# Attention V mixed with the mixing matrix stationary and gathered through DRAM, six exponent buffers, second mean on VectorE

## The chip, the cores and the metric

The kernel runs on one core of a Trainium2 chip. The metric is the device time of one execution in microseconds (us). Most executions of one kernel agree within a few tenths of a per cent; one of the first three of the kernel before took 669 us, is far outside, and is not used. Where kernels are compared, the runs were made in turns on the same chip and only runs of the fast state count.

## The reference, cut to what matters

Four batches of attention with eight heads, 768 tokens and 64 columns. The tokens fall into 8 blocks of 96, and a Sinkhorn-normalised 8 x 8 matrix P for each batch and head mixes the blocks of K and V before block-local attention. The result goes through a Fourier mix, a layer norm and a feed-forward network (512 to 2048 to 512).

```python
for _ in range(5):
    P = P - np.max(P, axis=-1, keepdims=True); P = np.exp(P)
    P = P / (np.sum(P, axis=-1, keepdims=True) + 1e-09)
    P = P / (np.sum(P, axis=-2, keepdims=True) + 1e-09)
k_sorted = np.einsum('bhij,bhjcd->bhicd', P, k_b)
v_sorted = np.einsum('bhij,bhjcd->bhicd', P, v_b)      # the change is about this line
attn = softmax(scale * q_b @ k_sorted.T)               # in blocks of 96
out = attn @ v_sorted                                  # then Fourier mix, layer norm, FFN
```

## The kernel before

A list scheduler in Python orders all operations ahead of time from estimated costs; every engine then works through its own list in order. V comes in two halves: batches 0 and 1, then 2 and 3. V arrives with (batch, head, block) on the 128 partitions. The products need the 96 tokens of a block on partitions. The kernel before gets there on TensorE: V is copied so that 96 tokens of one column d lie side by side, that piece is the stationary operand, and the mixing matrix `bd` streams past it.

```python
# V's path, t = 0 or 1 for the half
for hf in range(2):                       # mean over tokens, on TensorE
    for n in range(6):
        nc.tensor.matmul(psm.ap, idh, nat[t][:, 3072*hf + 512*n : ... + 512], ...)
V.tensor_reduce(vb[:, 0, :], psm.ap.rearrange("p (c d) -> p d c", d=D), ...)
# ... 8 pieces: t=0 a copy, t=1 minus the mean, both to "p (d r c)"
V.tensor_tensor(dst, src, vbn[...].broadcast_to([128, 16, 6, 8]), op=ALU.subtract)
# mixing: 64 stationary operands, 128 columns stream past each
nc.tensor.matmul(o, vcx[:, 96*d : 96*d + m], bd, ...)
copy(e, vsb[0:96, :, 4*n : 4*n + 4], ps.ap[0:96].rearrange("p (d g) -> p g d", d=4))
# ...
# exponent buffers, zeroed once by GpSimd
for n in range(4):
    nc.gpsimd.memset(eb4[0:96, n, :], 0.0)
# layer norm's small steps on GpSimd, between the loads that GpSimd issues
G.tensor_scalar(mv.ap[:, :, 1], mv.ap[:, :, 1], 1e-6, None, op0=ALU.add)
# results of the second token group go out by GpSimd's row scatter
nc.gpsimd.indirect_dma_start(out..., bass.IndirectOffsetOnAxis(ap=rows[:, i:i+1], axis=0), u.ap, None)
```

Loads with a cast from float32 to float16 are issued by GpSimd. So GpSimd's one list holds loads, buffer fills, layer-norm steps and row scatters.

The softmax here doesn't subtract the row's maximum and nothing guards it: scores larger than these inputs give would overflow.

## Time and profile before

| | before |
|---|---|
| time, two runs | 290.75 and 292.56 us |
| first feed-forward product (ff1) starts | 70.25 us |
| last product's result added | 281.57 us |
| TensorE / VectorE / ScalarE / GpSimd busy | 260.9 / 171.9 / 157.9 / 66.3 us |

Busy time by engine, and two of the 40 slices that the prediction does not show, from the page of the kernel before (7.25 us a slice, busy share in tenths):

```profile
PE 260.9 (90%) x2284; PEld 155.2 (54%) x2284; DVE 171.9 (59%) x405; ACT 157.9 (54%) x323; POOL 66.3 (23%) x104
...
POOL 8973300015900640011220002032000212200021
PEclk9997999998899999999999999999999999999997
```

GpSimd (POOL) is empty in the sixth to eighth slice and nearly so in the ninth, up to 65 us, just before the layer norm of batch 0 falls due at 64 us, and TensorE's granted clock (PEclk) is under 8 tenths in one slice only, the fourth. When that layer norm falls due, GpSimd is waiting for its statistics, not they for it (start, us, instruction, idle before it and what ended it):

```profile
64.33 0.26 POOL L1193 TENSOR_SCALAR mv<-mv 128x3 f32<-128x3 f32 x1 [25.71 <-DVE mv L1188]
```

I use one more quantity, TensorE's **lag**: the time at some point minus the work that TensorE has done up to it. The work is each matmul in its list times the steady spacing of its shape, 0.162 us for 384 columns and so on, as the prediction derives them. Counted row by row by one rule for all kernels, it is 236.9 us before. The lag is 34.3 us when ff1 starts and 44.6 at the end. It grows where TensorE waits or runs at half clock.

### The profile page before, as it was taken

To read this page: it belongs to the slowest core of one execution; us is meant where nothing else is said; L and a number is where in the kernel's file an instruction comes from. 1 tells how busy PE (TensorE), PEld (TensorE's weight loads), DVE (VectorE), ACT (ScalarE), POOL (GpSimd) and SP (SyncE) were. 2 spreads that over 40 slices of the span, in tenths; PEclk is the share of its full clock that TensorE was granted. 3 is DMA by queue.
4 is the path that set the end of the run, shared out by engine and by line. 5 is a ranking of instruction groups with operands and counts; after the bars stand their busy time and mean duration, and the time that the engine had idled before them with its cause. 6 is when DMAs were issued, how large, how long until landed. Compare 5 with 4: busy or idle time off the path is not lost.

```text
span 290.0 us, 5807 instructions
## 1 busy us (share of the span) xinstructions
PE 260.9 (90%) x2284; PEld 155.2 (54%) x2284; DVE 171.9 (59%) x405; ACT 157.9 (54%) x323; POOL 66.3 (23%) x104
## 2 busy tenths in 40 slices
PE   0389988897999999999999999999999999999980
PEld 0258866554565656554566456455555546545530
DVE  4697999999999999831579643145034226210020
ACT  2677979785778945970477037137415505425300
POOL 8973300015900640011220002032000212200021
PEclk9997999998899999999999999999999999999997
DMA  7999999910990897211113010311311111221001
GB/s 114 211 260 245 215 208 211 219 37 5 157 146 10 95 165 133 66 37 20 77 47 57 36 52 22 58 72 50 57 72 37 38 54 72 38 90 36 2 36 72
DMA packets 42529, 26.33 MB, mean 91 GB/s; under 512 B 30106, under 2 KB 38824, under 8 KB 42500
## 3 DMA queue, kind: packets, MB, share of 16 engines
q0 software_dynamic: 23536, 18.31, 37.4%
q1 hardware_dynamic: 18966, 7.64, 11.6%
q8 instruction: 18, 0.29, 0.4%
q14 instruction: 9, 0.07, 0.1%
HBM read 28.96 MB, written 6.29 MB: 122 GB/s over the span
## 4 chain that ended last, share of the span: by engine, by line
PE 62%; DVE 22%; DMA 8%; issue 3%; POOL 2%; ACT 1%; POOLq 0%; DVEq 0%
PE bank L1253 26%; PE bank L1274 25%; DMA hr<-in_v_dram 4%; DVE vsf L660 3%; DVE vcx L708 3%; DVE rt L1006 3%; DMA out_dram<-u,rows 2%; POOL kq L472 2%; DMA kq<-in_q_dram 2%; PE bank L1149 2%; PE bank L991 2%; DVE st L1186 1%; PE bank L952 1%; PE bank L897 1%; DVE ks L660 1%
## 5 line engine op out<-in xcount | busy, mean ns | idle before, releaser
L1265 ACT ACTIVATE hr<-bank 128x384 f16<-128x384 f32 x115 | 56.3, 491 | 75.2 <-PE bank L1253 74.4
L1253 PE MATMUL bank<-ut,w1sb 128*128 128x384 f16 x512 | 92.8, 329 | 0.7 <-ACT ut L660 0.7
L1274 PE MATMUL bank<-w2sb,hr 128*128 128x512 f16 x384 | 87.9, 379 | 0.0
L1253 PEld LDWEIGHTS <-w1sb 128*128 128x128 f16 x512 | 49.0, 99 | 34.8 <-issue 1.8
L1274 PEld LDWEIGHTS <-hr 128*128 128x128 f16 x384 | 36.7, 98 | 41.8 <-issue 0.2
L1282 DVE TENSOR_TENSOR u<-bank,u 128x512 f32<-128x512 f32 x24 | 16.5, 689 | 60.2 <-PE bank L1274 59.8
L961 ACT ACTIVATE ex<-bank 96x384 f32<-96x384 f32 x64 | 27.9, 485 | 6.3 <-PE bank L952 6.0
L1295 POOL DMA_INDIRECT out_dram<-u,rows x12 | 12.2, 1013 | 77.0 <-DVE u L1282 56.7
L1193 POOL TENSOR_SCALAR mv<-mv 128x3 f32<-128x3 f32 x8 | 1.9, 240 | 109.8 <-DVE mv L1188 109.8
L976 ACT ACTIVATE eb<-ex,negone 96x384 f16<-96x384 f32 x35 | 20.8, 615 | 0.2
L1213 ACT ACTIVATE un<-u,nm,ny 128x512 f16<-128x512 f32 x15 | 12.2, 810 | 11.8 <-DMA ut<-un 8.5
L1172 DVE SCALAR_TENSOR_TENSOR u<-rt,bank 128x510 f32<-128x510 f16 x12 | 8.1, 678 | 16.3 <-PE bank L1138 8.9
L991 PE MATMUL bank<-vsf,eb 97*128 97x65 f16 x416 | 16.5, 193 | 1.3 <-DVE rr L836 0.5
L1006 DVE TENSOR_TENSOR rt<-bank,rz 128x384 f16<-128x384 f32 x32 | 17.2, 549 | 0.3
L991 PEld LDWEIGHTS <-eb 97*128 97x128 f16 x416 | 15.4, 98 | 3.6 <-issue 1.3
L472 POOL DMA_DIRECT2D kq<-in_q_dram x20 | 16.4, 850 | 1.7 <-DMA kq<-in_q_dram 1.2
L1186 DVE BATCH_NORM_STATS2 st<-u 128x6 f32<-128x512 f32 x24 | 16.1, 686 | 0.3
L1160 DVE SCALAR_TENSOR_TENSOR u<-rt,bank 128x512 f32<-128x512 f16 x12 | 8.0, 684 | 13.9 <-PE bank L1153 13.5
L927 PE MATMUL bank<-pack,qr 128*128 128x128 f16 x48 | 4.8, 246 | 12.3 <-ACT qr L660 11.7
L724 PE MATMUL bank<-bdv,vcx 128*128 128x128 f16 (+1 forms) x128 | 12.6, 225 | 0.0
L952 PE MATMUL bank<-qt,ks 64*128 64x96 f16 x256 | 11.3, 207 | 1.3 <-DVE rt L1006 0.4
L897 PE MATMUL bank<-bdk,kq 128*64 128x128 f16 x192 | 10.7, 228 | 1.6 <-DVE bdk L636 0.8
(130 smaller groups left out, 338.2 us busy)
## 6 DMA issues: line engine op xcount, KB each, us to landing
kq<-in_k_dram POOLq DMA_DIRECT2D x8, 384.0 KB, 6.6
w1sb<-in_moe_w_ch_dram POOLq DMA_DIRECT2D x4, 512.0 KB, 16.0
w2sb<-in_moe_w_ch_dram POOLq DMA_DIRECT2D x4, 512.0 KB, 19.0
out_dram<-u SPq DMA_DIRECT2D x8, 256.0 KB, 2.0
kq<-in_q_dram POOLq DMA_DIRECT2D x4, 384.0 KB, 11.6
hr<-in_v_dram POOLq DMA_DIRECT2D x2, 768.0 KB, 11.2
kq<-in_v_dram POOLq DMA_DIRECT2D x2, 768.0 KB, 21.5
kq<-in_q_dram POOLq DMA_DIRECT2D x16, 96.0 KB, 5.5
```

The source lines that it names most:

```text
L472: o = P.add({eng: c}, lambda _: e.dma_start(dst, src), r=r, w=w, prio=prio, nbytes=nbytes, tag="load", after=after)
L897: nc.tensor.matmul(ps.ap[64 * h2:64 * h2 + 64, 128 * r3:128 * r3 + 128], k16[:, 2 * hl + h2, 3 * half + r3, :], bdk[:, 2 * hp + h2].rearra ...
L952: nc.tensor.matmul(pss[h2].ap[:, BLK * j:BLK * j + BLK], ks.ap[rows, 4 * g + j, :], qt.ap[rows, c0:c0 + BLK])
L961: nc.scalar.activation(ex.ap, pss[h2].ap[0:96, 0:384], AF.Exp, scale=SCALE),
L976: nc.scalar.activation(ed, src, AF.Identity, bias=negone[0:96])
L991: nc.tensor.matmul(po.ap[:, 65 * T:65 * T + 65], eb.ap[:, e0:e0 + 128], vsf[:, vi:vi + 65], start=(n == 0), stop=(n == len(WIN[T]) - 1), s ...
L1006: P.add({"DVE": (0.45, 0.56)}, lambda _: V.tensor_tensor(rt.ap[:, :, D * h:D * h + D], po3()[:, :, 0:D], rz.ap[:, :, None].broadcast_to([1 ...
L1186: P.add({"DVE": (0.6, 0.69)}, lambda _, u=u, st=st: V.bn_stats(st.ap, u.ap), r=[u], w=[st], tag="bn")
L1253: nc.tensor.matmul(ps.ap[:, 0:GT], w1sb[:, c, 128 * fc:128 * fc + 128], ut.ap[:, c, :], start=(c == 0), stop=(c == 3))
L1265: nc.scalar.activation(hr[g][:, fc, :], ps.ap[:, 0:GT], AF.Relu)
L1274: nc.tensor.matmul(ps.ap, hr[g][:, fc, 128 * tt:128 * tt + 128], w2sb[:, fc, :], start=(fc == 0), stop=(fc == 15))
L1282: V.tensor_tensor(u.ap, ps.ap, u.ap, op=ALU.add),
```

## The change

Its intent: no copies of V, fewer and larger products, contiguous evictions. The mixing matrix becomes stationary and V streams past it, 512 columns at a time. The result still has (batch, head, block) on partitions; it is stored to DRAM and gathered back with tokens on partitions. The gathers stand on GpSimd's list, the load queue. Two more exponent buffers are to bridge the trip, and the second half's mean moves to VectorE.

```diff
+VW = 80
+NEB = 6
...
+            for n in range(4):                      # second half's mean
+                P.add({"DVE": (1.65, 1.75)}, lambda _, n=n: V.tensor_reduce(
+                    vb[:, 0, 16 * n:16 * n + 16],
+                    n3.rearrange("p c d -> p d c")[:, 16 * n:16 * n + 16],
+                    axis=AX.X, op=ALU.add), ...)
...
+        for hf in range(2):                         # centring, in place
+                V.tensor_tensor(m, m, vbn[:, None, :].broadcast_to([128, 48, D]), op=ALU.subtract)
...
-                    nc.tensor.matmul(o, vcx[:, 96 * d:96 * d + m], bd, ...)
+                nc.tensor.matmul(o, bd, n4[:, r, 8 * hf:8 * hf + 8], start=True, stop=(t == 1))
...
+                      nc.sync.dma_start(vdr[t][w64, cols], vm[w64, cols]),
...
+                          nc.gpsimd.dma_start(
+                              vsb[32 * k_:32 * k_ + 32, w64, 0:D],
+                              vdr[t][w64, cols].rearrange("g (c d) -> c g d", d=D)),
...
+    gate = gets[0, 0][-1:]                          # tables and weights behind the first gathers
```

Less visible parts: V is loaded first, its second half in six pieces instead of two; the pieces that spread the mixing matrix are split into a high and a low half.

## The prediction

> **What bounds the kernel now.** I read the page's slices first, then the chain that ended last, then busy time by stage, then the groups by shape, then the timelines of VectorE and TensorE. The page's 40 slices (7.25 us each, tenths busy):
> ```profile
> PE   0389988897999999999999999999999999999980
> ...
> DVE  4697999999999999831579643145034226210020
> ACT  2677979785778945970477037137415505425300
> ...
> DMA  7999999910990897211113010311311111221001
> ```
> VectorE (DVE) is full from the fourth slice to the sixteenth, TensorE (PE) from the ninth to the end. The transfers are dense to about 58 us. Busy time by stage (a stretch in us, its length, then PE, PEld, DVE, ACT, POOL busy):
> ```profile
> 27.00:66.00 39.00, 34.18 (x581) 26.64 (x579) 38.39 (x95) 33.78 (x73) 4.86 (x10) 1.00 0.96 176
> 66.00:92.00 26.00, 23.74 (x208) 15.37 (x207) 25.11 (x61) 18.97 (x38) 10.31 (x15) 0.93 0.84 85
> 92.00:115.00 23.00, 22.55 (x305) 13.77 (x302) 22.56 (x49) 16.04 (x35) 8.09 (x10) 1.00 1.03 122
> 115.00:277.00 162.00, 161.89 (x1055) 87.98 (x1050) 65.43 (x148) 73.11 (x152) 18.68 (x33) 1.00 0.19 50
> ```
> From 27 to 66 us VectorE works 38.4 of 39 us: this front is VectorE's. From 115 to 277 us TensorE is busy 161.9 of 162 and VectorE 40%: that part is TensorE's. The chain of work that ended last says the same (start, us, what), with the start of the first feed-forward product, ff1, and the end of the last product:
> ```profile
> 36.43 0.62 DVE rr L836
> 37.32 0.47 DVE rt L1006
> ...
> 70.25 2.14 PE bank L1253 x8
> ...
> 277.24 0.70 DVE u L1282
> ```
> So the end is: TensorE's work, plus the time it has nothing to do, plus 12.8 us of closing (277.2 to 290.0). Busy time overstates its work, as matmuls overlap, so I count work by the steady spacing of blocks in the chain: 24 ff1 matmuls in 3.90 us (0.162 each), 36 ff2 in 7.77 (0.216), 26 attention matmuls in 0.80 (0.031), 16 of V's mixing in about 0.9 (0.056). Multiplied over the instruction order of TensorE this gives 240 us in all, 38.3 before the first ff1 and 56.4 before the first ff2 (which runs at 92.6 us). TensorE is thus without work for 70.25 - 38.3 = 32 us before ff1, 36 us by 92.6, and 277.2 - 240 = 37 us in all. The gain can come from two terms only: the 240, and the 37.
>
> **What the Trainium skill says, and whether the trace agrees.** "VectorE: DVE Perf Modes", The perf-mode tier table: a tensor_tensor on 16-bit SBUF operands reaches 2x, a tensor_reduce[...] 1x. The trace agrees for a dense one (pmt, 768 elements, 545 ns, against 800 ns for one element a cycle at the page's 0.96 GHz) and shows that the strided centring of V does not (768 elements in 1473 ns). "TensorE: Matmul & The Clock Gate", Back-to-back issue gap: N/2.4 + 2.5 ns, so 128 columns 56 ns and 512 columns 216; the blocks above agree with both. "DMA: Bandwidth & Descriptors", Anatomy of one DMA: some 2 us fixed in each transfer, and (Specifications) pieces under 512 B are slow. Here a plain 256 KB store lands in 2.0 us, and q loads of 768 rows of 256 B (96 KB) in 5.5. "SBUF — State Buffer", Terms: VectorE and GpSimd exclude each other on a shared port pair, which could delay the gathers' descriptors; no view of the kernel before shows that.
>
> **The change, part by part.** The groups by shape that it touches (busy us, mean ns):
> ```profile
> L724 PE MATMUL bank<-bdv,vcx 128*128 128x128 f16 x126 | 12.4, 225 | 0.0
> L708 DVE TENSOR_TENSOR vcx<-kq,vbn 128x768 f16<-128x768 f16 x8 | 11.7, 1473 | 0.0
> L660 ACT CAST vsf<-bank 96x512 f16<-96x512 f32 x16 | 11.6, 791 | 0.4 <-PE bank L724 0.3
> L660 DVE CAST vsf<-bank 96x512 f16<-96x512 f32 x16 | 11.4, 774 | 1.2 <-PE bank L727 1.1
> ...
> L727 PE MATMUL bank<-bdv,vbn 128*128 128x128 f16 x63 | 8.3, 231 | 0.0
> ...
> L660 DVE COPY vcx<-hr 128x768 f16<-128x768 f16 x5 | 4.5, 941 | 0.7 <-DMA hr<-in_v_dram 0.7
> L660 ACT COPY vcx<-hr 128x768 f16<-128x768 f16 x3 | 4.5, 1499 | 0.2 <-DMA hr<-in_v_dram 0.2
> ...
> L675 PE MATMUL bank<-kq,pack 128*128 128x512 f16 x12 | 2.9, 380 | 0.0
> ```
> *TensorE.* Out: 128 + 64 mixing matmuls of 128 columns at 0.056 = 10.8 us, the 12 of the second mean at 0.216 = 2.6, eight fp32 ones (about 1.3). In: 36 of 512 columns at 0.216 = 7.8, and 24 small fp16 ones (about 1.2). Net -5.7 us. All of it counts, since TensorE's work adds up to the end: the new order sums to 234.3.
>
> *VectorE.* I take durations from like rows and counts from the two instruction orders. Out: 16 evictions 11.4, centring 11.7, copies 4.1 (0.8 apart), one PSUM mean 0.7, small 1.3: 29. In: 9 evictions of 512 contiguous at about 0.62 = 5.6; two centrings of 3072 at 2x, 3072/1.92 GHz + 0.06 = 1.66 each, 3.3; four reductions of 1536 at 1x, 1.66 each, 6.6; four more exponent shifts and six more ReLUs taken from ScalarE (4.5); two q copies and the split of the mixing matrix in two halves (2.5): 22.5. Net -6.6 us. *ScalarE:* 16 evictions and 3 copies out, 15 evictions at 0.55 in, 10 pieces handed to VectorE: about -14 us.
>
> *Before the first normalised tile.* VectorE's order up to it (66.2 us in the kernel before) loses 5 copies (4.1), 10 evictions against 5 (3.7), 4 head norms and a matrix copy of the next batch (3.7), gains about 2.7: 8.8 us less. Also, one Sinkhorn exponential waited 2 us for q's copy on ScalarE; now the five run together, 1.76 us an iteration, so the mixing matrix is ready at about 11.6 instead of 14.3 us.
>
> *The new wait.* V is loaded first. Its halves landed 3.7 us apart (12.7 and 16.4) after k and q; without those (3.7 us together) I expect 9.0 and 12.7. Behind V, q lands at 14.6 and k at 16.4, and TensorE's order has q's transposes and one product of k ahead of the mixing: start 17.4. 12 steps of 0.43 and evictions end near 23. The last store of the first half is out at 23.5 and lands at 27. A gather moves 2048 rows of 128 B; two k loads and eight q loads (6144 rows) took 10.7 us (70.9 to 81.6), less 3.7 for k is 1.14 ns a row, so 2.3 us a gather, plus 2 fixed: last gather at 32 to 34 us. The six exponent buffers let three pairs of heads be ready by then. VectorE's own order ahead of the first head norm, 17.6 us from 17.4, says 35. The kernel before did that norm at 36.3. So the round trip costs about nothing, and from the norm to the first normalised tile VectorE has 22.8 us of work left (30 before). First ff1: 35 + 22.8 + 1 + 4 (66.2 to 70.25 before) = 62.8.
>
> *Sum.* Idle before ff1: 62.8 - 32.6 (work in the new order) = 30.2, so 1.8 less. Idle after it was 5 us; with looser engines I take 3.5. Work -5.7. In all -9 us: 292.6 to 283.5.
>
> **The rivals.** (1) **The round trip becomes the wait.** Stores and gathers meet k, q and the tables in queues that were full to 58 us; if the last gather lands at 38 or 40, ff1 starts at 67 and the gain falls to 5 us or less: 287 to 289. For it: dense transfers, 12,288 tiny rows a half. Against: tables and weights are held behind the first gathers. (2) **Weights arrive late.** They are issued after the gathers, some 10 us later than now (21.5 to 33 us). By bytes I expect w1 by about 54 and w2 by 63 us, in time; if not, ff1 waits: 286 to 290. (3) **GpSimd's in-order queue.** Gathers of the second half stand ahead of the row scatters of batch 0 and between layer-norm steps; a late store would hold those and, through the six u buffers, TensorE: 1 to 4 us at about 100 us. (4) **More gain.** The front was VectorE's from 27 on; if it simply shifts by 8.8 us and the 5 us behind it vanish, 277 to 280.
>
> **Range and chances.** The work term (-5.7) is firm to a microsecond. The start of ff1 is loose by 3 us either way, the stalls behind by 2. Quadratically some 4 us; with rival 3 the upper side is longer: 277 to 290. Faster by over 2% means under 286.7, 3.2 us above the centre: 0.69. Slower by 2% (298) needs a stall that I don't see: 0.05.
>
> **What would show it.** Right: first ff1 near 63 us and first head norm near 35; V's 36 mixing matmuls 0.216 apart; centring near 1.7 us; VectorE near 165 and ScalarE near 144 us busy; no TensorE gap of a microsecond after ff1. Wrong: TensorE's first attention product waiting for a gather with VectorE idle (rival 1), ff1 waiting for a weight transfer (2), a vector step waiting for a scatter (3), or a centring or reduction of V far above 1.7 us.

## The result, and the profile after

The changed kernel took 305.7 us (305.39 to 306.31, four runs) against 291.5 us (290.75 to 292.56, three runs, the one of 669 us left out) of the kernel before in the same rounds. The ratio is 1.0486, 95% interval 1.044 to 1.0532: slower. Ratios here are the mean time of one kernel's fast runs over that of the other's of the same rounds, so not quite the ratio of the medians.

| | before | predicted | after |
|---|---|---|---|
| time, us | 291.5 | 283.5 | 305.7 |
| TensorE's work, us | 236.9 | 5.7 less | 231.8 |
| first head norm, us | 36.3 | 35 | 39.8 |
| first ff1, us | 70.25 | 62.8 | 76.59 |
| lag at first ff1 / at the end, us | 34.3 / 44.6 | | 45.8 / 63.3 |
| VectorE / ScalarE busy, us | 172 / 158 | 165 / 144 | 177 / 146 |

The work fell as predicted, by 5.1 us. The lag rose by 18.7. Page of the changed kernel, busy time and slices of 7.6 us:

```profile
PE 259.8 (86%) x2124; PEld 147.1 (49%) x2124; DVE 176.8 (58%) x405; ACT 145.7 (48%) x307; POOL 87.6 (29%) x122
...
PE   0569786824999999799699999999999999999990
...
DVE  5898999735799999755599914316414315310020
...
POOL 8941953445820006762112000212200212200012
PEclk9979797985799999999799999999999999999996
DMA  7996999999990436999421111131221032131001
```

VectorE was full from 29 to 116 us before; now it has a hole in the ninth to eleventh slice, 61 to 83 us, where TensorE drops to 2 and 4 tenths and its clock to 5 in one slice. GpSimd is busy there, and transfers are dense to 91 us (58 before). What TensorE waited for, from its waits (total us, times, longest):

```profile
PE bank L717 <- DMA hr<-in_v_dram: 9.9, 2, 8.9
PE bank L1304 <- DVE u L1253: 8.4, 1, 8.4
PE bank L664 <- DVE fo L643: 3.0, 1, 3.0
PE bank L1325 <- DVE u L1354: 2.9, 2, 2.6
PE bank L1020 <- ACT ex L1029: 1.9, 2, 1.7
```

The first is V's first load, from the start. The other four are the places to look into. Three readings give a cause each.

**The layer norm.** The 8.4 us are a wait for the first normalised tile. GpSimd's timeline of the changed kernel (start, us, instruction, idle before it):

```profile
67.98 1.14 POOL L486 DMA_DIRECT2D kq<-in_v_dram  x1 [1.57 <-DMA w2sb<-in_moe_w_ch_dram]
69.20 0.25 POOL L1265 TENSOR_SCALAR mv<-mv 128x3 f32<-128x3 f32 x1
```

The statistics of batch 0's first group were complete near 61.8 us. The layer norm's first step starts at 69.20, right after the last of six loads of V's second half. Those stand ahead of it in GpSimd's list, and they wait for earlier weight loads: five of the six are issued about 0.5 us after one of these lands (54.6 and 55.1, 57.1 and 57.6, 62.0 and 62.6, 64.7 and 65.3, 67.4 and 68.0 us). Afterwards TensorE runs at half clock. Busy time by stage (length, then TensorE, weight loads, VectorE, ScalarE, GpSimd, then the granted clock, transfer share and GB/s):

```profile
60.00:70.00 10.00, 2.31 (x54) 1.87 (x53) 3.62 (x9) 2.81 (x7) 5.29 (x6) 0.82 1.23 209
70.00:80.00 10.00, 7.52 (x79) 5.44 (x80) 7.04 (x22) 4.87 (x8) 6.26 (x12) 0.50 2.33 162
```

**The start.** The Sinkhorn iterations ended at 11.5 us, as predicted. The next instruction on VectorE spreads the matrix with a copy, and takes 5.80 us. From the two engines' timelines:

```profile
11.55 5.80 DVE L643 COPY fo<-rv 32x1024 f16<-32x1024 f16 x1
...
9.49 7.32 POOL L560 MEMSET eb<- 96x1672 f16 x5
```

Beside it GpSimd fills the exponent buffers, now six of them.

**The second half.** Groups by shape of the changed kernel (busy us, mean ns):

```profile
L706 DVE TENSOR_REDUCE vb<-kq 128x16 f32<-128x1536 f16 x4 | 11.0, 2780 | 0.0
L742 DVE TENSOR_TENSOR kq<-kq,vbn 128x3072 f16<-128x3072 f16 x2 | 3.5, 1759 | 0.0
```

Centring is what the prediction said (1.76 against 1.66 us); a reduction takes 2.78 us instead of 1.66. And from the chain that ended last, a row scatter of batch 0:

```profile
138.52 7.42 DMA out_dram<-u,rows
```

It took 7.42 us to land; the median of all is 2.8. VectorE waits for it because it frees a buffer, and TensorE waits for VectorE at 148 us.

### The profile page after: what moved, and what is told of

The parts are those of the page before. It is cut to its first block, busy times and chain, and to the rows that moved or that the text cites. A ratio compares the mean times of both kernels' runs of the same rounds, so it can differ in the third digit from the quotient of the medians.

```text
span 303.3 us, 5530 instructions
## 1 busy us (share of the span) xinstructions
PE 259.8 (86%) x2124; PEld 147.1 (49%) x2124; DVE 176.8 (58%) x405; ACT 145.7 (48%) x307; POOL 87.6 (29%) x122
## 4 chain that ended last, share of the span: by engine, by line
PE 47%; DMA 4%; DVE 1%; issue 1%; POOLq 0%; DVEq 0%
PE bank L1325 21%; PE bank L1346 20%; DMA out_dram<-u,rows 4%; PE bank L1220 1%; PE bank L1132 1%; PE bank L1059 1%; PE bank L1020 1%; PE bank L1224 1%; DVE u L1354 0%; POOLq L1465 0%; PE bank L965 0%; PE bank L1208 0%; PE bank L1137 0%; DVE u L1244 0%; PE bank L1142 0%
## 5 line engine op out<-in xcount | busy, mean ns | idle before, releaser
L1325 PE MATMUL bank<-ut,w1sb 128*128 128x384 f16 x512 | 94.5, 331 | 3.1 <-DVE u L1354 2.9
L1337 ACT ACTIVATE hr<-bank 128x384 f16<-128x384 f32 x109 | 53.3, 490 | 73.1 <-PE bank L1325 72.4
L1367 POOL DMA_INDIRECT out_dram<-u,rows x12 | 12.1, 1007 | 72.7 <-DVE u L1354 57.2
L787 POOL DMA_DIRECT2D vsf<-vdr x12 | 13.0, 1088 | 43.0 <-DMA vdr<-kq 31.1
L1044 ACT ACTIVATE eb<-ex,negone 96x384 f16<-96x384 f32 x31 | 18.5, 614 | 0.3
L1059 PE MATMUL bank<-vsf,eb 97*128 97x65 f16 x416 | 17.2, 198 | 1.4 <-DVE rt L1075 0.5
L1020 PE MATMUL bank<-qt,ks 64*128 64x96 f16 x256 | 12.4, 211 | 2.6 <-ACT ex L1029 1.9
L693 ACT CAST ks<-bank 128x384 f16<-128x384 f32 x18 | 8.1, 482 | 11.6 <-PE bank L965 11.0
```

Source lines behind the costliest of these rows:

```text
L787: nc.gpsimd.dma_start(vsb[32 * k_:32 * k_ + 32, w64, 0:D], vdr[t][w64, cols].rearrange("g (c d) -> c g d", d=D)),
L1020: nc.tensor.matmul(pss[h2].ap[:, BLK * j:BLK * j + BLK], ks.ap[rows, 4 * g + j, :], qt.ap[rows, c0:c0 + BLK])
L1044: nc.scalar.activation(ed, src, AF.Identity, bias=negone[0:96])
L1059: nc.tensor.matmul(po.ap[:, 65 * T:65 * T + 65], eb.ap[:, e0:e0 + 128], vsf[:, vi:vi + 65], start=(n == 0), stop=(n == len(WIN[T]) - 1), s ...
L1325: nc.tensor.matmul(ps.ap[:, 0:GT], w1sb[:, c, 128 * fc:128 * fc + 128], ut.ap[:, c, :], start=(c == 0), stop=(c == 3))
L1337: nc.scalar.activation(hr[g][:, fc, :], ps.ap[:, 0:GT], AF.Relu)
```

## The experiments

Four theories: (A) the layer norm is late by GpSimd's in-order list; (B) VectorE's copies and GpSimd's fills shut each other out; (C) the second mean on VectorE is on the path; (D) the second half's trip makes TensorE wait behind 100 us. The standing rival is the prediction's first: the trip as such, and full transfer queues, set the pace whatever is done about the lists. Sixteen kernels ran. Each ratio is to the kernel before, on the same chip in the same rounds.

### The spreading copy as a maximum (e1)

```diff
-        V.tensor_copy(pk..., phl[0]...broadcast)
+        V.tensor_tensor(pk..., phl[0]...broadcast, phl[0]...broadcast, op=ALU.max)
```

> The changed kernel with one instruction replaced: the copy on VectorE that spreads the mixing matrix (5.80 us at 11.55 us, beside GpSimd's fills of the exponent buffers) becomes an elementwise maximum of the matrix with itself, same result, two inputs. Every engine's order stays the same. Theory (the copy and the fills shut each other out): the maximum takes 1.1 to 1.4 us although the fills still run until 16.8, V's mixing starts near 17 instead of 20.6 us, the first head norm comes 3 to 4 us earlier than 39.84. Rival (the copy is slow by its shape, or the partition range is slow): still 5 us or more. The end: if GpSimd's queue holds the first layer norm (69.2 us) whatever VectorE does, the total moves by less than 2 us: 303.5 to 306; if the start is on the path, about 302.

Measured: ratio 1.0469 (1.0422 to 1.0517), first ff1 at 76.22 us. VectorE's timeline of this run:

```profile
11.72 1.21 DVE L643 TENSOR_TENSOR fo<-rv 32x1024 f16<-32x1024 f16 x1
13.35 3.72 DVE L655 COPY rr<-rv 32x1024 f16<-32x1024 f16 x1
```

Same size, same place, same fills beside it: 1.21 us. The next plain copy, which took 0.4 us in the changed kernel after the fills, now starts among them and takes 3.72, to 17.07. So (B) holds: a copy that meets the fills ends with them, whichever copy it is. This agrees with the Trainium skill, "SBUF — State Buffer", Who interferes with whom: a copy in a two-port mode and a GpSimd instruction exclude each other, and an instruction with two SBUF inputs contends only with a GpSimd instruction that reads SBUF; a fill reads nothing. The start gained less than I expected, since the second copy took the place of the first: mixing began at 19.5 us (17 expected, 20.6 without the edit), and the first head norm at 39.1, 0.7 us earlier instead of 3 to 4. The total did not move, as the layer norm stood at 68.8 us still.

### Layer norm ahead of V's loads (e2), and both (e3)

```diff
-        for o in P.schedule():
+        seq = P.schedule()
+        vl = [o for o in seq if o.n in vloads]      # the six loads of V's second half
+        seq = [o for o in seq if o not in vl]
+        at_ = seq.index(lns[0]) + 1                 # behind batch 0's first layer norm
+        seq[at_:at_] = vl
+        for o in seq:
```

No other engine's order changes.

> The changed kernel with the six loads of V's second half moved on GpSimd's queue to just behind the first layer norm of batch 0; every other order the same. Theory (the layer norm stood behind loads that waited for their turn in the transfer queue): the layer norm starts within 0.5 us of its statistics, near 62 instead of 69.2 us; the 8.4 us wait of TensorE for the first transposes falls to 1 to 2 us; TensorE keeps its full clock between 70 and 80 us (0.50 now); first ff1 near 68 instead of 76.6; total 296 to 299. Rival (weights late, or the statistics themselves late): first ff1 moves by under 3 us and the total stays at 303 to 306. Second rival: V then arrives late for its reductions at 90 us, and half of the gain is lost.

Measured: ratio 1.0292 (1.0233 to 1.035), first ff1 at 70.45 instead of 76.59 us. GpSimd's timeline:

```profile
63.14 0.25 POOL L1267 TENSOR_SCALAR mv<-mv 128x3 f32<-128x3 f32 x1 [8.80 <-DVE mv L1262]
...
65.19 6.94 POOL L486 DMA_DIRECT2D kq<-in_v_dram  x6 [0.22 <-issue]
```

Now GpSimd waits for the statistics, not they for it; TensorE's waits for the first tile are 1.4 and 1.1 us. (A) is shown. Its worth is 1.9%, some 5.7 us; I had expected 7 to 10, and a full clock between 70 and 80 us, where it was 0.83.

> Both edits of the two runs before in one kernel. Theory: the gains add, since with the queue freed the start is on the path: first ff1 near 64 to 65 us, total 292 to 295. Rival (round trip of V through memory, or w1, w2 late, as the prediction's first and second rivals): first ff1 no earlier than with the queue edit alone.

Measured: ratio 1.0271 (1.0227 to 1.0314), first ff1 at 68.99. Together they gain little more than the queue edit alone. The expectation of 292 to 295 failed. The lag tells why: 38.2 us at ff1 and about 42 when the products of the third result tile are done (101.6 us; as much before, at 114.9), but 57.2 at the end (44.6 before). By then the front has been made up for; some 15 us are lost behind it.

### The second mean back on TensorE (e4), and alone on the kernel before (b7)

```diff
-            for n in range(4): ... V.tensor_reduce(... 1536 elements ...)
+            for hf in range(2): ... 6 x nc.tensor.matmul(psm.ap, idh, nat[t][... 512]) ...
```

> The changed kernel with one part undone: the second mean of V again as 12 products of 512 columns on TensorE and one reduction, instead of four reductions of 1536 elements on VectorE (11.0 us). Many orders behind 85 us change with it. If the VectorE reductions hold the path (VectorE is full from 90 to 104 us): VectorE 10 us less busy, idle of TensorE behind the first ff1 (12.4 us) down by 4 or more, total 301 to 303 in spite of 2.6 us more of TensorE's work. If they are hidden: 306 to 308, TensorE's added work.

Measured: ratio 1.0563 (1.0511 to 1.0616). The interval overlaps that of the changed kernel, but in the same rounds it took 309.8 us against 306.3 of e1, so nothing was gained. VectorE is 10.5 us less busy, V's second half is mixed by 110 us instead of 116. But TensorE meets a new wait of 3.9 us at 139.9 us. VectorE waited 4.4 us there for the transposes by transfer of batch 1's normalised tiles.

The same part alone, on the kernel before (the reverse edit):

> One part of the change alone, on the kernel before: the second mean as four reductions on VectorE instead of 12 products on TensorE. By the rows seen: 2.6 us of TensorE's work out, 11.0 us of VectorE's in, between 92 and 115 us where VectorE was busy 22.6 of 23 us. If VectorE has slack there that its order can use: 290 to 292. If V's second half, late by some 8 us, holds TensorE: 293 to 298.

Measured: ratio 1.0379 (1.0341 to 1.0417), about 11 us slower, beyond what I expected. The lists shift around it as well: ff1 starts 2 us later already, and the lag grows to 60.5 at the end. So the part is bad where it stands alone, and undoing it in the changed kernel does not give the time back. (C) can't be settled as a number that adds to others.

### No trip in the second half (e5)

The mean on TensorE, centring in place, V itself as the stationary operand at a stride of 128 bytes, evicted straight to tokens on partitions; e3's two edits kept.

```diff
+                        nc.tensor.matmul(ps.ap[0:128, 128 * dd:128 * dd + 128],
+                            kf[:, d:d + 64 * 127 + 1:64], bd, start=True, stop=True)
```

> The queue edit and the maximum instead of the spreading copy, as in the run with both edits, and in the second half of V no round trip: mean on TensorE, centring in place, then V itself as the stationary operand, read with a stride of 128 bytes (nothing copied), evicted straight to keys on partitions, as the kernel before has it. First half as in the changed kernel. Theory (the second round trip makes TensorE wait between 105 and 158 us: in the run with both edits TensorE falls 13 us behind its work there, the kernel before 3 to 4): it now falls behind by 4 to 6 us, no wait of a microsecond behind 100 us, total 292 to 295. Rival (the loss there comes from the finer interleaving of small products, not from the trip): still 10 us or more and 299 to 302. Side question: a strided stationary operand may load slower than the 106 to 117 ns of others; if it is over 200 ns, mixing is bound by it, 64 loads, some 7 us.

Measured: ratio 1.0386 (1.0306 to 1.0467). No gain in the total. Between 103 and 158 us TensorE falls some 10 us behind (by a recount of the lag), against 13.5 in e3 and 4 before; the theory wanted 4 to 6, the rival 10 or more. No wait of 1.4 us is left there, and the clock is full. The strided weight load takes 201 ns, dense ones of 128 columns 96 to 118. So the trip looks like a few microseconds of the loss behind 103 us, not like most of it, and (D) in its first form falls. The run also moves the mean and lengthens the weight loads, so it doesn't price the trip alone; the rival named in its expectation, the finer interleaving of small products, got no run of its own.

### The gathers of the second half left out (e6)

```diff
+        drop = gets[1, 0] + gets[1, 1]
+        seq = [o for o in seq if o not in drop]
```

Its output is wrong, which doesn't matter for the time.

> Wrong on purpose (batches 2 and 3 read the V of batches 0 and 1): the run with both edits, same order on every engine, with only the six gathers of the second half left out. It asks what the second trip's last step costs by itself. Theory: the 2.75 us wait of TensorE at 120 us, the half clock behind it and the slow landings of transposes and row scatters near 135 to 145 us go; TensorE falls behind by about 5 us instead of 13 between 103 and 158; total 292 to 295. Rival (the gathers are hidden; reductions, centring and stores are what costs): total within 2 us of 300.9. Output is wrong.

Measured: ratio 1.0306 (1.0234 to 1.0379), as with them. The gathers are hidden, and my theory was wrong. The run shows the wait more clearly, in three timelines (TensorE, ScalarE, the store queue):

```profile
125.77 0.85 PE L1024 MATMUL bank<-qt,ks 64*128 64x96 f16 x8 [4.52 <-ACT ex L1033]
...
124.53 0.81 ACT L1289 ACTIVATE un<-u,nm,ny 128x512 f16<-128x512 f32 x1 [5.66 <-DMA ut<-un]
...
116.18 10.38 SPq L1300 DMA_TRANSPOSE ut<-un  x3
```

TensorE waits for exponentials. They stand on ScalarE behind a normalisation, which waits for a tile buffer. The buffer is held by a transpose that a transfer does. Before, batch 3's k and q were loaded at 96 to 104 us. Here they run from 114 us, beside these transposes, because V's second half is staged in their slots until its last store.

### Batch 3's loads left out (e10), transposes on TensorE (e8)

> Wrong on purpose (batch 3 reads what lies in its k and q slots): the run with both edits, same order on every engine, with only the ten loads of k and q of batch 3 left out. New theory, after the gathers of the second half turned out to cost nothing: V's second half is staged in the slots that batch 3's k and q need, until its last store, so these loads run at 114 to 131 us instead of 96 to 104, just beside the transposes by transfer of batch 1's normalised tiles; these land late, ScalarE waits 5.7 us for a buffer of such a tile, the exponentials behind it wait, TensorE waits 2.7 to 4.5 us and runs at half clock behind. Theory: transposes land in under 3 us, TensorE's wait at 120 us goes, it falls behind by 5 to 7 us between 103 and 158 instead of 13; total 294 to 297. Rival (the tiles themselves are late, or there are too few buffers whatever the traffic): wait stays over 2 us, total 300 to 302. Output is wrong.

Measured (wrong results): ratio 1.0186 (1.0149 to 1.0224), 0.9% under e3 (on another chip). ScalarE still waits 3.9 us for a transpose, TensorE still 2.8 us at 125 us. The loads have a part in it; the wait does not go with them.

```diff
-            if b > 0:      # transposes by transfer
+            if b > 1:      # batch 1 on TensorE as well
```

> The run with both edits, with the normalised tiles of batch 1 transposed on TensorE as batch 0's are, instead of by transfers on the store queue (24 more products of 0.06 us, some 1.5 us of TensorE's work, six more evictions). Theory (the transfers' landing beside batch 3's loads holds ScalarE): ScalarE's wait for these transfers near 118 to 124 us goes, TensorE's wait for exponentials falls under 1 us, no half clock near 125, total 296 to 299. Rival (the wait only changes its name): 300 to 303.

Measured: ratio 1.0352 (1.032 to 1.0384). This is slower than e3. The rival was right: the wait changes its name. The wait near 123 us is gone, but TensorE waits 3.6 us at 144 us for VectorE, which waited 4.9 us at 141 for a row scatter.

### Six buffers against four (e7)

> The changed kernel with four exponent buffers instead of six. A dose for the theory that VectorE's copies and GpSimd's fills shut each other out: two fills of 1.5 us fewer, so the fills end near 13.9 instead of 16.8 us and the spreading copy that starts at 11.55 ends there too: 2.7 to 3.2 us instead of 5.8. If the copy is slow by itself it stays at 5.8. The total: with four buffers fewer pairs of heads are ready when the gathers land; if six buffers were worth what the prediction says, the first feed-forward product is late by 2 to 4 us although the start is 3 us earlier: 305 to 309; if they are worth nothing, 303 to 306.

Measured: 305.8 to 310.9 us, two of four runs slow, so no ratio. As a dose for (B) it is clean. VectorE's and GpSimd's timelines:

```profile
11.68 2.79 DVE L643 COPY fo<-rv 32x1024 f16<-32x1024 f16 x1
...
9.50 4.43 POOL L560 MEMSET eb<- 96x1672 f16 x3
```

Two fills fewer, and the copy ends at 14.47 instead of 17.35 us, still with the fills. In its profiled run the first attention product waits 4.5 us for a gather, which it did not with six buffers, not even in b3, where mixing started as early (17.2 against 17.6 us): they do bridge the trip. But ff1 came at 72.06 us, 4.5 us earlier than with six buffers, where I had expected it 2 to 4 us later.

### Candidates: both maxima (b3), and the scatter ahead of four loads (b5)

b3 is e8 with the second spreading copy as a maximum and three tile buffers.

> A candidate for a better kernel: as the TensorE-transposes run, with the second spreading copy of the mixing matrix as a maximum too (it took 3.72 us beside the fills) and three buffers of normalised tiles. Expected: mixing of the first half starts another 2 us earlier, first head norm at 36 to 37 us, first feed-forward product at 66 to 67, total 293 to 297. If the landing of stores and gathers in full queues sets the start, the norm stays at 38 to 39 and the total within 1 us of the TensorE-transposes run.

Measured: ratio 1.0227 (1.02 to 1.0253). First head norm at 35.5 us, first ff1 at 66.7: in this run the front is as early as expected, and the total is not. The profiled runs of b4, b5 and b6, with both maxima too, had the norm at 37.5 to 38.6 and ff1 at 67.9 to 69.8, although b5's lists are the same up to there: one profiled run places the front to 2 or 3 us, no better. b5 changes one place in GpSimd's list:

```diff
+        sc = next(o for o in seq if o.tag == "out" and o.eng == "POOL")   # first row scatter
+        # ... the last four q loads of batch 3 go behind it
```

> The candidate with the two maximum instructions, transposes on TensorE and three tile buffers, and one change of GpSimd's order: the first row scatter of batch 0 stands ahead of the last four q loads of batch 3 instead of behind them. In that candidate the tile was ready at 126.1 us, the scatter issued at 128.7 and landed near 136.6 (7.9 us, median 2.7), VectorE waited 6.5 us for its buffer, TensorE 5.2 us and ran at half clock behind. Theory (the prediction's third rival, the in-order queue, and the loads' traffic beside it): scatter issued near 126.4, lands by 130 to 132, TensorE's wait at 132 to 138 us falls to 0 to 2 us, no half clock, total 292 to 296 (299.5 without). Rival (scatters land late whatever stands before them): wait of 4 us or more, total 298 to 300.

Measured: 293.7 us, ratio 1.0009 (0.9978 to 1.0041), level with the kernel before. GpSimd and VectorE in b3:

```profile
128.70 1.09 POOL L1376 DMA_INDIRECT out_dram<-u,rows  x1 [0.30 <-issue]
...
136.67 0.69 DVE L1253 SCALAR_TENSOR_TENSOR u<-rt,bank 128x510 f32<-128x510 f16 x1 [6.54 <-DMA out_dram<-u,rows]
```

and in b5:

```profile
128.81 1.14 POOL L1376 DMA_INDIRECT out_dram<-u,rows  x1 [3.40 <-DVE u L1363]
...
133.80 0.69 DVE L1253 SCALAR_TENSOR_TENSOR u<-rt,bank 128x510 f32<-128x510 f16 x1 [1.23 <-DMA out_dram<-u,rows]
```

The scatter is issued at the same time by the clock only because b5's profiled run is 2.5 us later from the first head norm on. Its tile was ready at 126.1 us in b3, 2.6 us before the issue, and at 128.5 in b5, 0.3 us before. Behind all eight q loads the scatter then lands after 7.9 us, behind four of them by 5.0. So some 2.3 us are the list, and 3 us how long the transfer takes to land beside the others. VectorE waits 1.2 instead of 6.5 us, TensorE's wait of 5.2 us goes. The step from 1.0227 to 1.0009 is some 6.4 us for moving one instruction, by two runs on two chips. This is the prediction's third rival, twice over: once with the layer norm, once with the scatter, though behind loads and not behind gathers.

### The second mean on TensorE in the repaired kernel (b4, b6)

> The candidate before, with the second mean on TensorE again (12 products of 512 columns, 2.6 us, for 11.0 us of VectorE). With the waits behind it gone, the mean's place should show: if VectorE's reductions delay V's second half and with it batch 3's loads, stores and gathers 6 us earlier are worth more than 2.6 us: 290 to 295. If they were hidden: 2 to 3 us slower than the candidate before.

> The second mean on TensorE with both maximum instructions, layer norm ahead of V's loads, transposes on TensorE and three tile buffers, as before (299.4), and the instruction lists made with the second half's gathers taken as 8 us slower, so that TensorE meets the first attention product of batch 2 after 79.5 instead of 71.9 us of its work. In the run without, TensorE waited 2.1 us there for a gather and fell 2.5 us behind at 118 us. If lists made for the gathers as they are settle it: no wait for a gather behind 100 us, 291 to 296, that is at or under the kernel before. If other waits follow it: 297 to 300.

> The same with the gathers taken as 12 us slower (first attention product of batch 2 after 84.2 us of TensorE's work). Expected within 1 us of the run with 8 us if the wait for the gather is gone in both; more than 2 us slower if the later products then meet the row scatters.

Measured: 1.0242 (1.0199 to 1.0285), 1.0173 (1.0112 to 1.0235) and 1.018 (1.0076 to 1.0283). b4 equals b3 within the intervals. It has no late scatter, since its lists differ, but waits 2.1 us for a gather. Lists made for slower gathers take that wait away and gain at most 0.7%, which is not clear of the intervals; TensorE then waits 3.7 us for a normalised tile. None is under b5.

### The kernel before with V stationary at a stride (b2)

> Not a part of the change but what it points to: the kernel before, with V itself as the stationary operand in both halves, read with a stride, so that no copy of V is made (8 copies of 768 elements, 9.0 us over VectorE and ScalarE, go; the centring of the second half is done in place in two instructions of 1.76 us instead of eight of 1.47). No trip through memory. V is loaded in six pieces a half. If a strided stationary operand loads as fast as a dense one: VectorE some 12 us less busy, first ff1 at 66 to 69 us instead of 70.25, total 286 to 291. If it loads slowly, or the finer pieces land later than 17 us, no gain or a loss: 292 to 297.

Measured: ratio 1.0548 (1.0474 to 1.0621); the profiled run was slow, so I compare only its weight loads with each other. Groups of weight loads:

```profile
L725 PEld LDWEIGHTS <-hr 128*96 128x96 f16 x64 | 13.9, 239 | 0.2
L725 PEld LDWEIGHTS <-kq 128*96 128x96 f16 x64 | 10.6, 257 | 0.7 <-DVE kq L709 0.7
L728 PEld LDWEIGHTS <-vbn 128*96 128x96 f16 x64 | 8.8, 138 | 0.0
```

96 columns at a stride of 128 bytes take 239 to 257 ns; with one element repeated they take 138, and dense ones took 123 in the kernel before, longer than 128 columns (101). V also came in finer pieces. How much is whose I did not separate. A miss: no kernel beats the kernel before.

## Why the prediction was wrong, point by point

**TensorE's work** was right: 5.1 us less by one count, 5.7 predicted, and V's products ran 0.215 apart.

**The start** was wrong in one term. The Sinkhorn matrix was ready at 11.5 us (predicted 11.6); "start 17.4" for the mixing was 20.6. The spreading copy was taken at its 0.67 us of the kernel before, where it ran after the fills. Now it ran among them and took 5.80. The prediction named the shared port pair, looked for it in transfers alone, and dropped it as "no view of the kernel before shows that". VectorE's copies did show it: in the kernel before, a copy of 768 elements beside the fills took 1.32 us (12.92 to 14.25, the last fill ending at 14.29), the next, after them, 0.80. The move that brought the copy into the fills was its own: a Sinkhorn 2.7 us earlier and two fills more. With both copies as maxima the head norm was at 35.5 in b3 (predicted 35) and at 37.5 to 38.6 in b4, b5 and b6, so the rest of that step, the trip included, was off by 0.5 to 3.6 us.

**"First ff1: 35 + 22.8 + 1 + 4 = 62.8"** was 76.6: in the same terms 39.8 + 23.8 + 7.5 + 5.5. VectorE's 22.8 was nearly right: its work ran out at 63.6. The first term is the start above. The step that failed is the "+ 1": VectorE then stood idle for 7.5 us until the first normalised tile (71.1), as the layer norm, whose statistics were ready at 61.8, stood behind V's loads on GpSimd until 69.2. The rival "GpSimd's in-order queue" named the mechanism, but placed it at 100 us with 1 to 4 us. The list of GpSimd's order was there to be read before predicting; the loads' waits for earlier loads were not put in time. In b3, with list and copies repaired, the terms are 35.5, then 23.2 to the layer norm's first step, then 8.0 instead of 5 (5.9 before) to ff1 at 66.7. In these 8 us the granted clock was 0.66 and 0.50 (62 to 66, 66 to 70 us); before, it was 1.00 in both stretches. That is where the last 3 us lie; no run took the half clock away, so it is not shown that they come from it.

**"Reductions 1.66 each"** were 2.78. The table that the prediction names ("VectorE: DVE Perf Modes", The perf-mode tier table) rates a reduction at 1x, which the prediction took as one element a cycle; this one steps 128 bytes from element to element. "SBUF — State Buffer", in the note on cachelines of Door 1: The DMA port swizzle, says that consecutive accesses within 16 bytes run at full bandwidth and that each new line costs extra; the trace agrees, with 1.81 ns an element. The prediction had the strided centring at 1473 ns for 768 in hand, 1.92 ns an element, and did not apply it. VectorE's busy time shows both errors: 176.8 against 165, of which 4.4 are the reductions and 5.1 the copy.

**"Idle after it 3.5"** was 17.5 by the lag (63.3 - 45.8; 10.3 before by the same rule). The "5 us" that it started from was itself misread: 277.24 us is the third last of the added results, the last is at 281.57, so that its own sum gives 281.6 - 240 = 41.6 in all and 9.6 after ff1, and the closing is 8.5 us instead of 12.8. The prediction took V's second half as work only. It did not ask what its slots hold up: batch 3's loads moved from 96 to 114 us and later, and met the transposes and the row scatters. The repairs show the chain in part: without the transposes the scatter held TensorE, and with the scatter ahead of four loads the wait went.

**The other rivals.** The trip as such (first) was not the wait in the first half: 12 us from the last mixing product to the first attention product in b3, against 9 to 11 predicted. That product did start within 0.4 us of the last gather's landing (38.3 us in the changed kernel, 34.2 in b3), but VectorE was idle by then for 0.7 us at most. The gather's own term was near by luck: the ten loads that it was taken from landed by 84.6, not 81.6, which by the same sum gives 3.3 us a gather instead of 2.3, and the gathers landed 1.7 to 2.2 us apart. In the second half leaving out its gathers changed nothing. The weights (second) came later than predicted (w1 by 62 and w2 by 72.5 us, 54 and 63 predicted), but no run shows TensorE waiting for them at ff1.

**What stays open:** where the rest of the loss behind 103 us goes. From 103 to 158 us TensorE is busy 54.3 of 55 us at a clock of 1.00 in b5, as it is before (54.5), and yet by a recount of the lag it falls 7.7 us behind there, 3.7 before; it runs 648 products instead of 574. The finer interleaving of small products is a rival for these 4 us that no run tested. Also open: why the second mean costs 11 us alone on the kernel before and nothing can be had by undoing it here; how much of the slow transposes is traffic; and the last 3 us ahead of ff1.

## What to carry to other kernels

When a change adds instructions to an engine that issues transfers and also does small steps on the path, write that engine's list down in time, with what each issue waits for. A 0.25 us step behind six waiting loads cost 5.7 us, more than half of the 9 that the change was to gain. Moving work earlier changes what it runs beside, so a duration taken from a row holds only with the same neighbour. And ask of every buffer that the change keeps longer what load it holds up, and what that load will then meet.

## What the Trainium skill lacked or had wrong

- "VectorE: DVE Perf Modes", the perf-mode tier table: it gives tensor_reduce 1x without a word on stride. A reduction of 1536 two-byte elements at a stride of 128 bytes took 2.78 us, 1.81 ns an element. "SBUF — State Buffer" has the cacheline note, but no figure for VectorE.
- "SBUF — State Buffer", Who interferes with whom: who shuts out whom agrees with every run. The rule speaks of a block for one instruction; what it lacks is a run of them. GpSimd's fills overlap (each starts 0.18 us before the one ahead ends), and a copy of 1024 elements, 0.4 to 0.7 us alone, took 5.80, 3.72 and 2.79 us, to the end of all of them. A maximum with two inputs in its place took 1.21.
- "DMA: Bandwidth & Descriptors": no page says what loads that wait in GpSimd's list cost the small steps and scatters behind them. Here a layer-norm step stood about 7 us behind six waiting loads, and a row scatter right behind eight q loads landed after 5.8 to 7.9 us in six runs, 4.0 with those loads left out (e10), 2.7 to 2.8 at the median.
- "TensorE: Matmul & The Clock Gate", LDWEIGHTS: no figure for a strided stationary operand. 128 columns at 128 bytes took 201 ns against 96 to 118 dense; 96 columns took 239 to 257 against 138 with one element repeated.
